# Output product of a recurrent step: the attention output held stationary and the weights moving in two 64-column tiles, instead of the weights held stationary

## The chip, the cores and the metric

The kernel runs on one core of one Trainium2 chip. The metric is device time in microseconds (us) of the whole program. Before the change three runs give a median of 2348.43 us (2343.58 to 2348.47).

## The reference, cut to what matters

Two branches are mixed by a gate. Branch A is sliding-window attention over 2048 tokens of width 640. Branch B is recurrent: it walks through the 2048 tokens in 64 segments of 32, and each segment sees 8 memory tokens that the segment before it made.

```python
g = sigmoid((x * gate_w).sum(-1, keepdims=True))
a = A_ref(x, A_wqkv, A_wo)            # window of 256, 32 heads of 20
mem = mem0                            # 8 tokens of width 640
for s in range(64):                   # branch B
    h = concat([mem, x[32 * s:32 * s + 32]])           # 40 tokens
    q, k, v = h @ Wq, h @ Wk, h @ Wv                   # 32 heads of 192
    p = softmax(mask(q @ k.T * 192 ** -0.5))
    o = (p @ v).reshape(40, 6144) @ Wo                 # 6144 x 640
    mem, b = o[:8], o[8:]
out = g * a + (1 - g) * b
```

## The kernel before, in words

**Stages.** `branch_A` runs first, and while it runs the program begins to load branch B's weights. `tail_projections` then works out, for all segments at once, the part of q, k and v that belongs to the last 8 tokens of each segment and puts it into DRAM (`xin`). What is left for the recurrent loop, `branch_B`, is 32 tokens a step: 8 of memory and 24 of the segment. A step is a chain: everything in it needs the memory that the step before made at its very end.

**Weights.** The four weight matrices of branch B do not fit into SBUF. They are cut into pieces of 128 x 1536 (384 KB), five to each of the four head groups of q, k, v and o. 58 pieces stay in SBUF for the whole loop; the 22 named in `STREAMED` are loaded anew in each step by the SP queue into a ring of six buffers, tag `w`. A buffer is free again when TensorE has used it up.

**A step's work for one head group g (0 to 3).** `chunk` makes q, k and v: the 32 tokens `hT` are stationary in four 32-column tiles, and 384 columns of weights move (line 747). ScalarE copies the result out. `turn` transposes q and k (line 771). GpSimd copies the tail tokens in (`b_K`, `b_Kz`, `b_QT`). `scores` multiplies them (lines 818 and 825), VectorE and ScalarE make the softmax, `turn_p` transposes it (877, 879), `values` multiplies with v (907, 914), and ScalarE copies the result to `OT` (918), which has the head dimension on the partitions and 40 tokens for each of 12 blocks.

**The output product.** `oproj` (line 934) holds a 128 x 128 block of Wo stationary and moves the 40 tokens of `OT` past it: 60 weight loads and 60 products a head group, 240 a step, with the output width on the partitions (`ps_o`, five blocks of 40 tokens). After the last one VectorE copies the 8 memory tokens straight into the next step's `hT` (line 945), since they stand there transposed already. ScalarE copies the other 32 tokens to `oT` (950).

**The rows out.** In the next step, `store` (name `x` in the order) turns `oT` back by five transposes (962), VectorE adds the gated branch A (971), and GpSimd's queue stores the sum (975, 976), loads the rows of branch A for the following segment into the only buffer `ga` (966, 967) and keeps a copy in `b_dram` (964). That load has to wait until the stores before it have landed, and what stands behind it in GpSimd's queue waits with it.

**The order.** TensorE's order within a step is the string `STEP`, written out by hand; q, k, v and o of a group are a word each, `tq`, `tk` the transposes, `s` scores, `p` the transpose of the softmax, `pv` the values. `Sched.run` puts the instructions of all other engines in place by estimated times. The products have a tile mode each: 32 columns (q, k, v, `x`), 64 columns (`tq`, `tk`, `s`, `p`, `pv`), 128 columns (o). The string before changes between modes 19 times a step.

Of the kernel before, what the change touches and what calls it, by code (L numbers as in the profile page):

```python
# [14 lines left out]
SEG = 32  # L15
# [5 lines left out]
def branch_A(tc, x, wqkv, wo, gate_w, ga_dram, spread_x=None, omg_dram=None, omg_sb=None, rl_all=None, exact=False, extra_units=None, W=256, HA=32):  # L21
# [17 lines left out]
    with ExitStack() as ctx:  # L39
# [8 lines left out]
        wq3 = wqkv.rearrange("(kt p) n -> p kt n", p=P)  # L48
# [12 lines left out]
        with tc.tile_pool(name=f"{n_}_wstage", bufs=KT) as wsp:  # L61
# [7 lines left out]
            with nc.allow_non_contiguous_dma(reason="tiny gate vector"):  # L69
                nc.sync.dma_start(gw[:], gate_w.rearrange("(kt p) -> p kt", p=P))  # L70
# [36 lines left out]
        def prep_units(qb):  # L107
            stt = {}

            def u_x():  # L110
                xt = xts.pop(qb)
                tp = ps_p.tile([P, KT, P], BF, name="xT_ps", tag="p")
                for kt in range(KT):
                    nc.tensor.transpose(tp[:, kt, :], xt[:, kt * P:(kt + 1) * P], ident[:])
# [57 lines left out]
        def finish_units(qb):  # L172
# [10 lines left out]
            def u_o(c0, c1):  # L183
# [8 lines left out]
                if c1 == D:  # L192
                    if exact:
                        nc.sync.dma_start(ga_dram[qb * P:(qb + 1) * P, :], ga[:])
                    else:
                        nc.sync.dma_start(ga_dram[:, qb * P:(qb + 1) * P, :].rearrange("k t d -> t k d"), ga[:].rearrange("p (k d) -> p k d", d=P))
# [124 lines left out]
        if omg_dram is not None:  # L321
            with nc.allow_non_contiguous_dma(reason="tiny omg vector"):
                nc.sync.dma_start(omg_dram.rearrange("(b p) -> p b", p=P), omg_all[:])
            for k in range(4):
                for i in range(4):
                    dst = omg_sb[SEG * k:SEG * k + SEG, :].rearrange("p (b i) -> p b i", i=4)[:, :, i]
                    nc.gpsimd.tensor_copy(dst, omg_all[SEG * i:SEG * i + SEG, :])


def mix(tc, b_dram, ga_dram, omg_dram, outf):  # L330
    nc = tc.nc
    nseg = b_dram.shape[0]
    with ExitStack() as ctx:
        one = ctx.enter_context(tc.tile_pool(name="m_c", bufs=1))
        sb = ctx.enter_context(tc.tile_pool(name="m_sb", bufs=2))
        ps = ctx.enter_context(tc.tile_pool(name="m_ps", bufs=2, space=bass.MemoryType.PSUM))
        ident = one.tile([P, P], BF, name="m_ident")
        make_identity(nc, ident[:])
        omg = one.tile([SEG, nseg], FP32, name="m_omg")
        with nc.allow_non_contiguous_dma(reason="tiny omg vector"):  # L340
            nc.sync.dma_start(omg[:], omg_dram[:].rearrange("(s t) -> t s", t=SEG))
        for s in range(nseg):
            bT = sb.tile([P, KT * SEG], BF, name="m_bT")
            nc.sync.dma_start(bT[:], b_dram[s])
            ga = sb.tile([SEG, D], BF, name="m_ga")
            nc.sync.dma_start(ga[:], ga_dram[s * SEG:(s + 1) * SEG, :])
            t = ps.tile([SEG, KT, P], BF, name="m_t")
            for kt in range(KT):
                nc.tensor.transpose(t[:, kt, :], bT[:, kt * SEG:(kt + 1) * SEG], ident[:])
            nc.vector.scalar_tensor_tensor(out=ga[:], in0=t[:].rearrange("p k c -> p (k c)"), scalar=omg[:, s:s + 1], in1=ga[:],  # L350
                                           op0=ALU.mult, op1=ALU.add)
            nc.sync.dma_start(outf[s * SEG:(s + 1) * SEG, :], ga[:])
# [130 lines left out]
class Weights:  # L483


    def __init__(self, tc, Wq, Wk, Wv, Wo, streamed):
        self.tc, self.nc = tc, tc.nc
        self.W = {k: W.rearrange("(kt p) h e -> p kt (h e)", p=P) for k, W in (("q", Wq), ("k", Wk), ("v", Wv))}
# [4 lines left out]
    def load(self, u, dst, engine):  # L493
# [3 lines left out]
        elif m < 4:  # L497
            engine.dma_start(dst, self.Wo[:, 4 * g + m, 0:PIECE])
        else:
            engine.dma_start(dst.rearrange("p (r c) -> p r c", r=4), self.Wo[:, 4 * g:4 * g + 4, PIECE:1920])  # L500

    def load_resident(self, pool, u, engine):
        t = pool.tile([P, PIECE], BF, name=f"w_{u[0]}{u[1]}{u[2]}")
# [9 lines left out]


def o_blocks(m):

    if m < 4:
        return [(m, n // 5, n % 5, n * P) for n in range(12)]
# [612 lines left out]
```

## Time and profile before

| | |
|---|---|
| runs | 2343.58, 2348.43, 2348.47 us |
| the profiled execution | 2344.06 us, span 2342.3 us |
| busy share of the span | PE 86%, PE weight loads 65%, DVE 43%, ACT 39%, POOL 31% |
| mean granted TensorE clock | 0.925 of full speed |
| DMA traffic | 649.24 MB, mean 277 GB/s |
| chain that ended last | PE 67%, DMA 17%, issue 9%, ACT 3%, DVE 3% |
| q, k, v (line 747) on the chain | 23% of the span |
| output product (line 934) on the chain | 17% |

The loop takes the span from about 541 us to its end. A row of a view of groups reads: line, engine, operation, tile written and tiles read, shape, count, then the busy time in us and the mean duration of one in ns, then the idle time of the engine just before them and what ended it. "issue" is time in which the engine waited for nothing that the profile shows. PEclk is the granted TensorE clock as a share of full speed; the DMA share is the mean busy share of the core's 16 DMA engines.

### The profile page before, as it was taken

Reading aid. Unit: us, or ns where it says so; the run is one execution under the profiler, and the core shown is the slowest. Engines: PE = TensorE matmul, PEld = TensorE weight load, DVE = VectorE, ACT = ScalarE, POOL = GpSimd, SP = SyncE. Lnnn points to the kernel's source line nnn. Section 1 sums busy time; section 2 is a strip of 40 time slices with the busy share of each in tenths; the row PEclk is TensorE's granted clock in tenths of the full one; section 3 lists DMA queues with packets and bytes.
Section 4 is the critical chain, followed back from the end, with each engine's and each line's share of the span. In section 5 each row is a group of like instructions: output and inputs, shape, how many; then the busy total and the mean of one; then the engine's idle time right before and its main releaser. Section 6 shows DMA issues by size and latency. Waiting matters only on the chain.

```text
span 2342.3 us, 110323 instructions
## 1 busy us (share of the span) xinstructions
PE 2013.0 (86%) x48566; PEld 1513.0 (65%) x48566; DVE 1014.9 (43%) x3330; ACT 923.1 (39%) x1957; POOL 717.1 (31%) x1957
## 2 busy tenths in 40 slices
PE   6888888997888888888888888888888888888888
PEld 5777777854666666666666666666656666666666
DVE  4666663323444433344444443333334444434334
ACT  3556562223333333333333333333333333333333
POOL 3111121123333333333333333333333333333332
PEclk8778778998999999999999999999999999999999
DMA  3121226558999999999999999999999999999998
GB/s 113 61 67 54 60 63 214 159 170 301 324 329 345 321 336 334 331 329 333 335 333 342 315 335 329 325 326 315 336 313 320 327 328 338 347 316 314 332 332 286
DMA packets 293050, 649.24 MB, mean 277 GB/s; under 512 B 53064, under 2 KB 98768, under 8 KB 292560
## 3 DMA queue, kind: packets, MB, share of 16 engines
q1 hardware_dynamic: 254256, 587.84, 72.0%
q0 software_dynamic: 31392, 47.96, 7.4%
q8 instruction: 382, 6.26, 1.1%
q10 hardware_dynamic: 6912, 6.29, 0.9%
q14 instruction: 108, 0.88, 0.1%
HBM read 612.38 MB, written 29.37 MB: 274 GB/s over the span
## 4 chain that ended last, share of the span: by engine, by line
PE 67%; DMA 17%; issue 9%; ACT 3%; DVE 3%; POOL 0%; SPq 0%; ACTq 0%; POOLq 0%; DVEq 0%
PE ps_o L934 17%; PE ps_k L747 9%; DMA b_w<-in_B_Wv_dram 9%; PE ps_q L747 8%; PE ps_v L747 6%; PE qk_ps L132 5%; PE t_psum L550 4%; DMA b_w<-in_B_Wq_dram 4%; PE ps_pv L907 3%; ACT pt L223 2%; DMA b_w<-in_B_Wo_dram 2%; PE S_ps L825 2%; PE s_ps L220 2%; PE t_psv L573 2%; PE tr_q L771 1%
## 5 line engine op out<-in xcount | busy, mean ns | idle before, releaser
L747 PEld LDWEIGHTS <-b_hT 128*32 128x32 bf16 x15360 | 404.4, 99 | 344.5 <-issue 156.0
L934 PE MATMUL ps_o<-b_OT,w_o 128*128 128x40 bf16 x9984 | 340.0, 182 | 66.3 <-issue 65.9
L934 PEld LDWEIGHTS <-w_o 128*128 128x128 bf16 x9984 | 292.6, 97 | 79.1 <-issue 71.6
L747 PE MATMUL ps_k<-w_k,b_hT 128*32 128x384 bf16 x4352 | 256.8, 346 | 14.8 <-issue 14.5
L803 POOL COPY b_K<-b_xg 128x64 bf16<-128x64 bf16 x256 | 60.1, 235 | 640.8 <-PE S_ps L825 474.4
L747 PE MATMUL ps_v<-w_v,b_hT 128*32 128x384 bf16 x3840 | 240.1, 334 | 13.0 <-issue 12.4
L747 PE MATMUL ps_q<-w_q,b_hT 128*32 128x384 bf16 x3328 | 227.6, 341 | 13.7 <-issue 13.5
L918 ACT CAST b_OT<-ps_pv 128x480 bf16<-128x480 f32 x256 | 143.3, 560 | 232.0 <-PE ps_pv L914 150.2
L934 PE MATMUL ps_o<-b_OT,b_w 128*128 128x40 bf16 x5376 | 196.4, 181 | 44.3 <-issue 40.6
L223 ACT ACTIVATE pt<-s_ps 128x1024 bf16<-128x1024 f32 x180 | 180.8, 1023 | 129.9 <-PE s_ps L220 129.7
L758 ACT CAST b_tok<-ps_q 128x384 bf16<-128x384 f32 x256 | 122.7, 479 | 213.1 <-PE ps_q L747 203.9
L934 PEld LDWEIGHTS <-b_w 128*128 128x128 bf16 x5376 | 164.5, 97 | 49.7 <-issue 44.6
L747 PE MATMUL ps_q<-b_w,b_hT 128*32 128x384 bf16 x1792 | 161.2, 344 | 35.8 <-DVE b_hT L945 18.7
L794 DVE COPY b_K<-tr_k 128x256 bf16<-128x256 bf16 x256 | 72.4, 283 | 272.7 <-PE tr_k L771 268.1
L891 DVE TENSOR_TENSOR b_PTm<-PT_ps,mk_m 128x320 bf16<-128x320 f32 x256 | 125.2, 489 | 140.5 <-PE PT_ps L879 138.8
L758 ACT CAST b_vtok<-ps_v 128x384 bf16<-128x384 f32 x256 | 122.4, 478 | 145.5 <-PE ps_v L747 143.6
L945 DVE CAST b_hT<-ps_o 128x40 bf16<-128x40 f32 x63 | 12.5, 199 | 378.2 <-PE ps_o L934 378.2
L758 ACT CAST b_tok<-ps_k 128x384 bf16<-128x384 f32 x256 | 122.3, 478 | 128.6 <-PE ps_k L747 120.8
L225 DVE TENSOR_TENSOR pt<-pt,pat 128x1024 bf16<-128x1024 bf16 x180 | 124.3, 691 | 75.2 <-ACT pt L223 72.4
L708 POOL DMA_DIRECT2D b_xg<-xin x256 | 137.2, 536 | 62.3 <-POOL b_QT L784 37.9
L836 DVE TENSOR_REDUCE sm<-S_ps 128x4 f32<-128x160 f32 x256 | 80.4, 314 | 140.4 <-PE S_ps L825 139.2
L780 ACT COPY b_QT<-tr_q 128x384 bf16<-128x384 bf16 x256 | 123.7, 483 | 29.6 <-PE tr_q L771 28.9
(137 smaller groups left out, 3738.5 us busy)
## 6 DMA issues: line engine op xcount, KB each, us to landing
b_w<-in_B_Wq_dram SPq DMA_DIRECT2D x448, 384.0 KB, 5.3
b_w<-in_B_Wo_dram SPq DMA_DIRECT2D x448, 384.0 KB, 5.7
b_w<-in_B_Wv_dram SPq DMA_DIRECT2D x320, 384.0 KB, 5.9
b_w<-in_B_Wk_dram SPq DMA_DIRECT2D x192, 384.0 KB, 5.5
xin<-t_qk POOLq DMA_DIRECT2D x8, 1536.0 KB, 9.1
b_xg<-xin POOLq DMA_DIRECT2D x256, 48.0 KB, 5.1
w_k<-in_B_Wk_dram SPq DMA_DIRECT2D x17, 384.0 KB, 4.1
b_xv<-xin POOLq DMA_DIRECT2D x64, 96.0 KB, 5.0
```

The costliest lines, as they stand in the source:

```text
L132: nc.tensor.matmul(pst[:, gg, :], lhsT=Wp[:, kt, 4 * g:4 * g + 4, :].rearrange("p h d -> p (h d)"), rhs=stt['xT'][:, kt, :], start=(kt == ...
L223: nc.scalar.activation(out=pt, in_=sp[:], func=ACT.Exp, scale=scale)
L225: nc.vector.tensor_tensor(out=pt, in0=pt, in1=pat.unsqueeze(1).to_broadcast([P, 2, 512]), op=ALU.min)
L550: nc.tensor.matmul(pt[:, bb, :], lhsT=w[kt][:, c:c + P], rhs=xTb[:, kt, t0:t0 + HS * MEM], start=(x == 0), stop=(x == KT - 1))
L708: sc.op("DMA", 500, lambda: nc.gpsimd.dma_start(tile_of(b)[:].rearrange("p i b t -> p (i b t)"), xin[s, :, c:c + 192]), writes=[b])
L747: nc.tensor.matmul(t[32 * j:32 * j + 32, 0:384], lhsT=tile_of(hT)[:, kt, :], rhs=w[:, j * 384:(j + 1) * 384], start=(kt == 0), stop=(kt == ...
L758: nc.scalar.copy(dst, src)
L780: nc.scalar.copy(dst, tq["tile"][:].rearrange("p b (j t) -> p b j t", t=SEG))
L836: nc.vector.tensor_reduce(out=x["mx"][:], in_=view(), axis=AX.X, op=ALU.max)
L891: nc.vector.tensor_tensor(out=tile_of(PTm)[:], in0=src.to_broadcast([P, 2, 4, L]), in1=mk_m[:].unsqueeze(1).unsqueeze(3).to_broadcast([P, ...
L918: sc.op("ACT", act(480), lambda: nc.scalar.copy(tile_of(OT)[:].rearrange("p b j l -> p (b j l)"), o["tile"][:, 0:480]), reads=[o], writes= ...
L934: nc.tensor.matmul(t[:, dt * L:(dt + 1) * L], lhsT=w_of("o", g, m, wb)[:, c:c + P], rhs=OT["tile"][:, b, i, :], start=(g == 0 and m == 0 a ...
```

## The change

**The output product** is turned over. `OT` is stationary now, 64 columns of it (40 tokens and 24 columns that nobody reads), and 320 columns of Wo move. The two halves of the output width go to the two 64-column tiles of TensorE, so that `ps_o` holds tokens on partitions 0 to 39 and 64 to 103 and 320 columns each. That is 24 products of 320 columns a head group in place of 60 of 40 columns, in the 64-column mode. Wo's pieces are 128 x 1280 now (320 KB), six to a group.

**The memory** no longer stands transposed. VectorE copies all of `ps_o` to `osum` (128 x 320), then TensorE turns the 8 memory tokens by ten products with 8 columns of the identity (`finish`, name `m`, at the end of the step), and VectorE copies the result into `hT`. So that the strided columns `kt::KT` come out right, the rows of Wq, Wk, Wv, of branch A's weights and of x are taken in the order `(p kt)` and not `(kt p)`.

**The rows out** need no transposes: the step `x` with its five transposes, ScalarE's copy to `oT` and one of the two VectorE instructions are gone. One VectorE instruction of 128 x 320 mixes `osum` with `ga`. `osum`, `ga` and the copies are moved by two DMAs of 32 partitions each; the gate `omg_sb` is loaded from DRAM once, by two small DMAs after branch A.

**The order** is a new string with 14 changes of mode a step, and the streamed pieces are others: 14 of 384 KB (q 5, k 4, v 5) and 10 of 320 KB (o), against 22 of 384 KB (q 7, k 3, v 5, o 7).

```diff
-STEP = "q0 k0 k1 tq0 tk0 k2 q1 s0 tk1 tk2 q2 k3 tq1 v0 p0 tq2 s1 q3 v1 s2 tk3 tq3 pv0 v2 p1 s3 o0 pv1 p2 x v3 pv2 p3 o1 pv3 o2 o3"
+STEP = "k0 q0 k1 tk0 tq0 q1 k2 tq1 s0 tk1 k3 q2 s1 tk2 v0 q3 tq2 p0 v1 tk3 pv0 tq3 s2 v2 p1 s3 o0 pv1 p2 v3 pv2 p3 o1 pv3 o2 o3 m"
...
-            for i, b, dt, c in o_blocks(m):
-                nc.tensor.matmul(t[:, dt * L:(dt + 1) * L], lhsT=w_of("o", g, m, wb)[:, c:c + P], rhs=OT["tile"][:, b, i, :],
...
+            for n in range(2):
+                i, b = divmod(2 * m + n, 3)
+                c = (4 * b + i) * L
+                for h in range(2):
+                    w = w_of("o", g, m, wb)[:, n * D + h * (D // 2):n * D + (h + 1) * (D // 2)]
+                    nc.tensor.matmul(t[64 * h:64 * h + 64, 0:D // 2], lhsT=OT["tile"][:, c:c + 64], rhs=w,
...
+                                     tile_position=(0, 64 * h), skip_group_check=True)
...
+        osum = sc.buf("osum")
+        sc.op("DVE", dve(320), lambda: nc.vector.tensor_copy(tile_of(osum)[:], o_b["tile"][:, 0:D // 2]), reads=[o_b], writes=[osum])
...
+            for kt in range(KT):
+                for h in range(2):
+                    nc.tensor.matmul(t[64 * h:64 * h + 64, kt, :], lhsT=osum["tile"][:, kt::KT], rhs=ident[:, 64 * h:64 * h + MEM],
...
+            sc.op("DVE", dve(40), lambda: nc.vector.tensor_copy(tile_of(hT)[:, :, 0:MEM], b["tile"][:]), reads=[b], writes=[hT], after=[xl])
...
+        for h in range(2):
+            sc.op("DMA", 500, lambda h=h: nc.gpsimd.dma_start(half(b_dram, h), mine(osum["tile"], h)), reads=[osum])
+            sc.op("DMA", 500, lambda h=h: nc.gpsimd.dma_start(mine(tile_of(ga), h), half(ga_dram, h)), writes=[ga])
...
+            nc.vector.scalar_tensor_tensor(out=ga["tile"][:], in0=osum["tile"][:], scalar=omg_sb[:, s:s + 1], in1=ga["tile"][:],
...
+        for h in range(2):
+            sc.op("DMA", 500, lambda h=h: nc.gpsimd.dma_start(half(outf, h), mine(ga["tile"], h)), reads=[ga])
...
-            "o": ((3, 4), (1, 3), (1,), (0, 1))}
+            "o": ((0, 3, 5), (0, 3, 5), (0, 5), (3, 5))}
```

On TensorE, where a step ends and the next begins, this stands before (`ps_o` is the output product, `b_hT` the next step's tokens):

```order
L934 LDWEIGHTS w_o_8443
L934 MATMUL ps_o<-b_OT,w_o_8443 128x40
L747 LDWEIGHTS b_hT
L747 MATMUL ps_q<-b_w,b_hT 32x384
L747 LDWEIGHTS b_hT
```

and this at the same place now (`b_osum` is the copied output, `mem_ps` the turned memory; the ten pairs of line 940 are cut to the first):

```order
L920 LDWEIGHTS b_OT_6445
L920 MATMUL ps_o<-b_w,b_OT_6445 64x320
L940 LDWEIGHTS b_osum_6448
L940 MATMUL mem_ps<-ident,b_osum_6448 64x8
...
L729 LDWEIGHTS b_hT
L729 MATMUL ps_k<-w_k_737,b_hT 32x384
```

Ten weight loads and ten products have come between the last output product and the next step's first projection; what is stationary and what moves has changed places. From one step to the next TensorE has 1330 instructions before and 1052 now.

On VectorE the same place reads like this before:

```order
L891 TENSOR_TENSOR b_PTm<-PT_ps,mk_m 128x320
L886 TENSOR_TENSOR b_PTx_6453<-PT_ps,mk_x 64x128
L945 CAST b_hT<-ps_o 128x5x8
L794 COPY b_K_20360<-tr_k 128x8x32
L798 TENSOR_TENSOR b_Kz_6443<-tr_k,mk_z 128x8x32
```

and now:

```order
L873 TENSOR_TENSOR b_PTm<-PT_ps,mk_m 128x320
L868 TENSOR_TENSOR b_PTx_6442<-PT_ps,mk_x 64x128
L928 CAST b_osum_6448<-ps_o 128x320
L954 SCALAR_TENSOR_TENSOR b_ga_6450<-b_osum_6448,omg_sb,b_ga_6450 128x320
L945 CAST b_hT<-mem_ps 128x5x8
L776 COPY b_K_25924<-tr_k 128x8x32
```

The copy into `b_hT` has two instructions of 320 columns ahead of it: the copy to `osum`, and the mix, which needs `ga` from DRAM.

In GpSimd's queue the stores and loads of a step stand together now, at the step's end:

```order
L950 DMA b_dram<-b_osum_6448 32x320
L950 DMA b_dram<-b_osum_6448 32x320
L958 DMA out_dram<-b_ga_6450 32x320
L958 DMA out_dram<-b_ga_6450 32x320
L951 DMA b_ga_6450<-ga_dram 32x320
L951 DMA b_ga_6450<-ga_dram 32x320
L785 COPY b_K_16819<-b_xg 128x8x8
L787 COPY b_Kz_6432<-b_xg 64x4x8
```

The copies behind them are those of head group 2 of the step that has begun, whose buffers come free with that step's `s0`.

165 lines of the change are left out of this document (68 added, 97 removed).

## Prediction

> **What bounds the kernel now.** I begin with the length of a step. VectorE's copy of the memory into `b_hT` ends each step; the view of that line gives its first and last start, and a table by windows gives the busy times between them.
>
> ```profile
> L945 DVE CAST b_hT<-ps_o x63: 198/199/200, 575.9 to 2311.4; 128x40 bf16<-128x40 f32 x63
> ```
> ```profile
> 575.90:2311.40 1735.50, 1493.90 (x41230) 1094.26 (x41230) 710.97 (x2667) 661.69 (x1550) 595.32 (x1673) 0.96 0.95 329
> ```
> ```profile
> 660.95:688.24 27.29, 23.15 (x665) 17.26 (x665) 11.25 (x44) 10.68 (x25) 9.93 (x28) 1.00 0.99 353
> 1981.00:2071.00 90.00, 79.94 (x2212) 58.43 (x2215) 39.87 (x151) 36.60 (x87) 32.45 (x95) 0.96 0.98 343
> ```
>
> The columns are the window, its length, the busy time of PE, PEld, DVE, ACT and POOL, the clock, the DMA share and GB/s. 62 steps take 1735.5 us, 27.99 each, of which PE is busy 24.1. DVE, ACT and POOL are under half busy. The DMA engines are busy 0.95 of it and move 329 GB/s, 9.21 MB a step. So two resources are close together: TensorE with 3.9 us of idle time a step, and the DMA engines with 5%. The second fence is a single step and a 90-us stretch in which the DMA engines did better: 353 and 343 GB/s.
>
> What TensorE's idle time is, the groups of line 934 and the timeline of one output product say.
>
> ```profile
> L934 PE MATMUL ps_o<-b_OT,w_o 128*128 128x40 bf16 x9984 | 340.0, 182 | 66.3 <-issue 65.9
> L934 PE MATMUL ps_o<-b_OT,b_w 128*128 128x40 bf16 x5376 | 196.4, 181 | 44.3 <-issue 40.6 <-DMA b_w<-in_B_Wo_dram 3.2
> ```
> ```profile
> 1455.40 0.42 PE L934 MATMUL ps_o<-b_OT,w_o 128*128 128x40 bf16 x10 [0.55 <-issue]
> ...
> 1459.97 0.39 PE L934 MATMUL ps_o<-b_OT,b_w 128*128 128x40 bf16 x9 [0.49 <-issue]
> 1460.21 0.45 PE L934 MATMUL ps_o<-b_OT,w_o 128*128 128x40 bf16 x12
> 1460.59 0.40 PE L907 MATMUL ps_pv<-b_PTm,b_vtok 128*64 128x160 bf16 x6
> 1460.82 0.26 PE L914 MATMUL ps_pv<-b_PTx,b_xv 128*64 128x64 bf16 x6
> 1461.01 0.47 PE L934 MATMUL ps_o<-b_OT,w_o 128*128 128x40 bf16 x12
> 1461.33 0.45 PE L934 MATMUL ps_o<-b_OT,b_w 128*128 128x40 bf16 x12
> 1461.63 1.06 PE L934 MATMUL ps_o<-b_OT,w_o 128*128 128x40 bf16 x36
> 1462.53 0.76 PE L934 MATMUL ps_o<-b_OT,b_w 128*128 128x40 bf16 x24
> 1463.13 0.43 PE L934 MATMUL ps_o<-b_OT,w_o 128*128 128x40 bf16 x11
> 1465.63 0.79 PE L934 MATMUL ps_o<-b_OT,w_o 128*128 128x40 bf16 x25 [2.07 <-issue]
> ```
> ```profile
> q1 hardware_dynamic: 254256, 587.84, 72.0%
> ...
> q8 instruction: 382, 6.26, 1.1%
> ```
>
> Line 934 loses 65.9 + 40.6 = 106.5 us to "issue", 1.66 a step, and waits only 3.2 us for its weights. From the stall that ended at 1459.97 to the one that ended at 1465.63 TensorE ran 9+12+6+6+12+12+36+24+11 = 128 products, in the middle of a weight piece and of a block. Queue q8 carries 382 packets; TensorE has 48,566 products and as many loads, so a packet is 254 instructions: the 128 products with their loads. I read the stalls as TensorE having run through its block of instructions before the next had come through the crowded DMA engines. From stall to stall 5.66 us passed, 3.59 of them work: the fetch takes longer than 128 products of 40 columns do. The stall ahead of these ended at 1455.40, so the block in between took 4.57 us with a stall of 0.49: the fetch takes some 4.5 to 5.7 us.
>
> The stalls cost a second time.
>
> ```profile
> 1463.00:1466.40 3.40, 1.33 (x48) 1.15 (x44) 0.00 (x0) 0.00 (x0) 0.52 (x1) 0.99 1.02 366
> 1466.40:1469.80 3.40, 3.11 (x41) 1.61 (x44) 0.20 (x1) 0.77 (x2) 1.26 (x3) 0.50 0.74 221
> ```
>
> After 2.07 idle us in 3.4, the next 3.4 us have half the clock, and DMA falls to 0.74 as well, since buffers are not freed. A mean clock of 0.96 over the loop means 8% of it at half clock: up to 0.04 x 27.99 = 1.1 us of TensorE's time a step.
>
> **The change part by part**, us a step, TensorE's side first. The chain of waits gives the pieces:
>
> ```profile
> 1423.01 0.21 PE ps_pv L907 x6
> ...
> 1432.38 1.60 PE ps_o L934 x60
> ...
> 1437.53 0.02 issue
> 1437.55 0.21 DVE b_hT L945
> 1437.76 0.04 issue
> ...
> 1441.61 0.29 PE tr_q L771 x6
> 1441.90 0.17 PE tr_k L771 x6
> 1442.07 0.93 PE ps_k L747 x20
> 1443.00 0.81 PE ps_q L747 x20
> ...
> 1456.89 0.21 PE ox_ps L962 x5
> ```
>
> (a) *The output product itself.* Before, 60 products take 1.60, so 240 take 6.4. Now 48 pairs of 320 columns. Line 747 moves 384 columns in four tiles at once at 0.81/5 = 0.162 a group of four, which scales to 0.135 for 320; line 907 moves a pair of 160 in 0.07, which scales to 0.14. So 6.5 to 6.7: **+0.15** (0 to +0.3).
>
> (b) *Instruction stalls in it.* TensorE goes from 1330 to 1052 instructions a step, but what counts is the place: 128 products of the new shape last 64 x 0.135 = 8.6 us, longer than the fetch of 4.5 to 5.7. The 1.66 should go almost wholly: **-1.6** (0 to -1.66). The stalls elsewhere stay, since q, k, v and the scores run as before. [...]
>
> (c) *The half clock.* Part of the 1.1 goes with the stalls that bring it. The new pause at the step's end, (f), is shorter than the 2.07 above, but may sometimes do the same: **-0.6** (0 to -1.1).
>
> (d) *Mode changes.* `tr_q` behind `ps_k` takes 0.29, `tr_k` behind `tr_q` 0.17, `ps_k` behind a transpose 0.93, `ps_q` behind it 0.81: 0.12 a change. 19 become 14: **-0.6**.
>
> (e) *The five transposes* of line 962 go: **-0.2**.
>
> (f) *The end of the step*, where nothing else can run, because every product of the next step needs `hT`. Now 0.02 + 0.21 + 0.04 = 0.27 pass. The new chain is the copy of 128 x 320, the ten products, and then the same 0.27. The nearest rows:
>
> ```profile
> L891 DVE TENSOR_TENSOR b_PTm<-PT_ps,mk_m 128x320 bf16<-128x320 f32 x256 | 125.2, 489 | 140.5 <-PE PT_ps L879 138.8
> ...
> L805 POOL COPY b_Kz<-b_xg 64x32 bf16<-64x32 bf16 x512 | 106.2, 207 | 15.1
> ...
> L784 POOL COPY b_QT<-b_xg 128x96 bf16<-128x96 bf16 x256 | 67.3, 263 | 15.8
> ...
> L803 POOL COPY b_K<-b_xg 128x64 bf16<-128x64 bf16 x256 | 60.1, 235 | 640.8 <-PE S_ps L825 474.4 <-DMA b_xg<-xin 77.8 <-PE ps_o L934 20.5
> ...
> L976 POOL DMA_DIRECT2D out_dram<-b_ga x64 | 32.4, 506 | 1.7 <-issue 1.7
> ...
> L971 DVE SCALAR_TENSOR_TENSOR b_ga<-ox_ps,omg_sb,b_ga 128x128 bf16<-128x128 bf16 x64 | 21.9, 342 | 5.9 <-DMA b_ga<-ga_dram 5.3 <-PE ox_ps L962 0.5
> ...
> L191 DVE TENSOR_SCALAR ga<-out_ps,gcol 128x320 bf16<-128x320 f32 x32 | 17.4, 545 | 2.5 <-PE out_ps L189 2.4
> ```
>
> The copy costs about 0.5 (line 891: 489 ns; line 191: 545). The ten small products cost, from line 962 doubled, 0.4, with the way through the array and the semaphores about 0.6. The mix of 128 x 320 stands on VectorE between the two copies; at about 0.5 (342 ns for 128 columns, 489 to 545 for other instructions of 320) it runs beside the ten products and is covered; without that cover it would add 0.5. Together **+1.1** (+0.7 to +1.6). The mix also needs `ga`, whose load was issued a step earlier.
>
> GpSimd's queue: two copies to `b_dram`, two stores, then two loads that wait until the stores have landed, and behind them the tail copies for head group 2, for which `s2` waits.
>
> ```profile
> DMA to landing us min/median/max: 3.3/5.0/6.7
> ```
>
> That is the row of line 976's stores. Six issues of 0.5 (line 976, also 32 partitions), a landing of 5.0 and copies of 0.235 + 2 x 0.207 + 0.263 = 0.9 are 8.9 us, and with the 0.5 of the copy to `osum` they end 9.4 us into the step, 11.1 with a landing of 6.7. Ahead of `s2` stand 1.4 us of (f), ten projections of 0.81, six transposes of 0.17 and nine changes of 0.12, 11.6 us without the scores and values between them: covered, so nought (up to +0.3).
>
> Sum: 0.15 - 1.6 - 0.6 - 0.6 - 0.2 + 1.1 = -1.75: TensorE alone would allow 26.2.
>
> *The DMA's side.* Streamed weights go from 22 x 384 = 8448 KB to 14 x 384 + 10 x 320 = 8576 KB, +0.13 MB; instructions fall by 278 x 64 bytes (6.26 MB over 97,132), -0.02. Demand 9.32 MB a step. At 329 GB/s that is 28.3 us, at 343 27.2, at 353 26.4. Each is above TensorE's 26.2, so the DMA is late next: the gain of 1.75 is cut. I take 343, the rate of a stretch of three steps, since TensorE will hold the ring up less: **27.2**, 0.79 less than now, 64 x 0.79 = 51 us.
>
> Outside the loop I count nought: branch A's strided transposes are as many as before, and the small gate loads stand in GpSimd's queue where it was idle. Allow 5 us either way.
>
> The profiled execution took 2344.06 us, 2342.3 of them the span. 2344 - 51 = 2293; the median of the runs is 4.4 above that execution, so I forecast 2296.
>
> **The rivals.**
>
> *The DMA stays at its share (slower).* Place: the end of each step, where the ring of six fills while nothing is freed for 1.4 us. If the mean rate stays at 329 GB/s, a step is 28.3: +0.3 x 64 = +20, 2368. It decides where the rate stays under 9.32 MB / 27.99 us = 333. For it: the share is 0.95 already, and more bytes are asked for. Against: the windows show the share falling after TensorE's stalls, to 0.74, and 0.98 to 0.99 in good stretches. Chance 0.11.
>
> *The stalls are not the fetch (slower).* [...] Against it stand the 128 products. Chance 0.03.
>
> *The two column tiles don't run together (slower).* Then 96 x 0.135 = 13.0: 26.2 + 6.5 = 32.7, +300 us. Line 907's pairs, also in two tiles, speak against it. Chance 0.01.
>
> *Half the gain.* The rate rises to 337 GB/s only: 27.65, 2326. Chance 0.17; within 0.2% of now, 0.05.
>
> *The DMA gives way further.* At 353 GB/s as in the one step: 26.4, 2246. Chance 0.10. My forecast's own case (2275 to 2315) has 0.53.
>
> **How the numbers follow.** About 0.2% (4.7 us) is what a measurement of this kernel tells from no change. Faster: 0.53 + 0.17 + 0.10 = 0.80; same 0.05; slower 0.15. The range leaves out the slower cases (0.15) and the lower half of the last: 2262 to 2345.
>
> **What would show it.** Right: "issue" at the output product under 0.3 us a step, the loop's clock at 0.98, the DMA share at 0.97 or more with waits for weights in place of the stalls, and 1.3 to 1.5 us between the last output product and `ps_k`. Wrong: "issue" as large as now there; a rate at 329 GB/s; PE waiting for GpSimd's copies at `s2`; half-clock windows after each step's end.

## The result, and the profile after

| | before | changed |
|---|---|---|
| median (lowest to highest) | 2346.01 us (2337.42 to 2348.47, 4 runs) | 2273.48 us (2252.83 to 2276.28, 4 runs) |
| profiled execution, span | 2344.06 us, 2342.3 us | 2252.83 us, 2251.1 us |
| mean granted clock over the span | 0.925 | 0.952 |

The ratio is 0.9675, 95% interval 0.9621 to 0.9729, so 3.2% faster by the ratio; the medians lie 73 us apart. The forecast was 2296, the range 2262 to 2345. The profiled execution is the fastest of the four; the other three took 2271 to 2276, and a fifth execution on record, which is not in the median, took 2265.15.

The length of a step comes from the same two views as before, the line that ends a step and the table by windows over the loop (window, length, busy time of PE, PEld, DVE, ACT and POOL, clock, DMA share, GB/s):

```profile
L945 DVE CAST b_hT<-mem_ps x63: 198/199/201, 583.4 to 2219.2; 128x40 bf16<-128x40 f32 x63
```
```profile
583.40:2219.20 1635.80, 1479.65 (x32612) 1074.06 (x32612) 732.23 (x2666) 652.86 (x1488) 597.98 (x1736) 1.00 0.99 353
```

62 steps take 1635.8 us, 26.38 each, where they took 27.99. The clock rose from 0.96 to 1.00, the DMA share from 0.95 to 0.99, the rate from 329 to 353 GB/s; 353 x 26.38 is 9.3 MB a step, as forecast. So the DMA engines are full now. The loop gave back 1735.5 - 1635.8 = 99.7 us; the part ahead of the first `b_hT` became longer by 583.4 - 575.9 = 7.5, the part behind the last by 1.0, which leaves the 91.2 between the two profiled executions.

On the profile's page of the changed kernel, the instruction queue, the chain and the groups of the output product say what changed places:

```profile
q8 instruction: 313, 5.13, 0.9%
...
PE 54%; DMA 36%; DVE 4%; ACT 3%; issue 3%; POOL 0%; SPq 0%; ACTq 0%; DVEq 0%; POOLq 0%
...
L920 PE MATMUL ps_o<-b_w,b_OT 128*64 128x320 bf16 x2560 | 298.5, 301 | 49.8 <-DMA b_w<-in_B_Wo_dram 44.1
L920 PE MATMUL ps_o<-w_o,b_OT 128*64 128x320 bf16 x3584 | 330.0, 299 | 0.4 <-issue 0.3
```

"issue" ahead of the output product was 106.5 us; here it is 0.3 in one group, and the list of waits below has 3.0 for both. In its place stand 44.1 us of waiting for streamed pieces of Wo, where 3.2 stood. On the chain, issue went from 9% to 3% and DMA from 17% to 36%. The same in the list of TensorE's waits between 600 and 2150 us (total us, times, longest). First the kernel before, the larger of its waits for "issue", at the output product and elsewhere:

```profile
PE ps_o L934 <- issue: 95.4, 74, 2.6
...
PE ps_q L747 <- issue: 14.8, 14, 2.5
PE ps_k L747 <- issue: 14.3, 17, 1.5
...
PE ps_v L747 <- issue: 12.8, 14, 2.1
...
PE ps_pv L914 <- issue: 9.6, 6, 2.1
```

And the changed kernel, from the top of its list:

```profile
PE ps_o L920 <- DMA b_w<-in_B_Wo_dram: 41.2, 67, 1.9
PE mem_ps L940 <- DVE b_osum L928: 34.4, 59, 0.6
PE ps_v L729 <- DMA b_w<-in_B_Wv_dram: 19.1, 40, 1.3
PE ps_k L729 <- DVE b_hT L945: 17.5, 59, 0.3
PE ps_q L729 <- DMA b_w<-in_B_Wq_dram: 10.2, 18, 1.3
PE S_ps L807 <- issue: 4.6, 9, 1.1
...
PE ps_v L729 <- issue: 3.4, 6, 1.0
PE ps_o L920 <- issue: 3.0, 5, 1.3
PE ps_q L729 <- issue: 1.3, 2, 0.8
```

Waits for weights and the two waits of the step's end lead the list; waits for "issue" are single rows of a few us. What the reader should also see is in the lower rows of the first of these two fences: before, the projections and values lost 14.8 + 14.3 + 12.8 + 9.6 = 51.5 us to "issue" too (68.8 with the smaller rows elsewhere that are not shown), and most of that has gone as well, though those products themselves were not changed.

The end of a step, on the chain of waits (start, length, what):

```profile
1427.48 3.46 PE ps_o L920 x48
1430.94 0.02 issue
1430.97 0.50 DVE b_osum L928
1431.47 0.04 issue
1431.51 0.57 PE mem_ps L940 x7
1432.08 0.02 issue
1432.11 0.21 DVE b_hT L945
1432.32 0.04 issue
1432.36 1.00 PE ps_k L729 x20
```

From the last output product to the next projection 1.42 us pass, and the projections behind it run at full clock (20 products in 1.00; the granted clock is 1.00 from 1432.49 to 1435.90).

### The profile page after: what moved, and what is told of

It reads as the page before. It is cut to its first block, busy times and chain, and to the rows that moved or that the text cites. A ratio compares the mean times of both kernels' runs of the same rounds, so it can differ in the third digit from the quotient of the medians.

```text
span 2251.1 us, 92658 instructions
## 1 busy us (share of the span) xinstructions
PE 1995.3 (89%) x39670; PEld 1488.7 (66%) x39670; DVE 1036.5 (46%) x3330; ACT 914.3 (41%) x1893; POOL 717.5 (32%) x2011
## 4 chain that ended last, share of the span: by engine, by line
PE 54%; DMA 36%; DVE 4%; ACT 3%; issue 3%; POOL 0%; SPq 0%; ACTq 0%; DVEq 0%; POOLq 0%
DMA b_w<-in_B_Wo_dram 14%; DMA b_w<-in_B_Wv_dram 12%; PE ps_o L920 10%; PE ps_k L729 8%; DMA b_w<-in_B_Wk_dram 8%; PE ps_v L729 6%; PE ps_q L729 5%; PE qk_ps L132 5%; PE t_psum L538 4%; ACT pt L220 3%; PE S_ps L807 2%; PE tr_k L753 2%; PE tr_q L753 2%; PE s_ps L217 2%; PE ps_pv L889 1%
## 5 line engine op out<-in xcount | busy, mean ns | idle before, releaser
L729 PEld LDWEIGHTS <-b_hT 128*32 128x32 bf16 x15360 | 378.9, 97 | 291.4 <-issue 91.0
L920 PEld LDWEIGHTS <-b_OT 128*64 128x64 bf16 x6144 | 398.4, 110 | 78.6 <-issue 73.1
L920 PE MATMUL ps_o<-b_w,b_OT 128*64 128x320 bf16 x2560 | 298.5, 301 | 49.8 <-DMA b_w<-in_B_Wo_dram 44.1
L920 PE MATMUL ps_o<-w_o,b_OT 128*64 128x320 bf16 x3584 | 330.0, 299 | 0.4 <-issue 0.3
L729 PE MATMUL ps_q<-w_q,b_hT 128*32 128x384 bf16 x3840 | 237.0, 330 | 1.3 <-issue 1.3
L729 PE MATMUL ps_v<-w_v,b_hT 128*32 128x384 bf16 x3840 | 228.1, 328 | 2.3 <-issue 2.1
L776 DVE COPY b_K<-tr_k 128x256 bf16<-128x256 bf16 x256 | 73.3, 286 | 289.3 <-PE tr_k L753 288.4
L928 DVE CAST b_osum<-ps_o 128x320 bf16<-128x320 f32 x64 | 31.5, 492 | 351.5 <-PE ps_o L920 351.5
L753 PEld LDWEIGHTS <-b_tok 128*64 128x64 bf16 x3072 | 101.1, 110 | 94.1 <-ACT b_tok L740 40.9
L950 POOL DMA_DIRECT2D b_dram<-b_osum x128 | 64.4, 507 | 273.4 <-DVE b_osum L928 266.2
L951 POOL DMA_DIRECT2D b_ga<-ga_dram x128 | 63.8, 498 | 263.8 <-DMA out_dram<-b_ga 255.8
```

Source lines behind the costliest of these rows:

```text
L729: nc.tensor.matmul(t[32 * j:32 * j + 32, 0:384], lhsT=tile_of(hT)[:, kt, :], rhs=w[:, j * 384:(j + 1) * 384], start=(kt == 0), stop=(kt == ...
L753: nc.tensor.transpose(t[64 * a:64 * a + 64, k, :], tok["tile"][:, c:c + 64], ident[:], tile_position=(0, 64 * a))
L920: nc.tensor.matmul(t[64 * h:64 * h + 64, 0:D // 2], lhsT=OT["tile"][:, c:c + 64], rhs=w, start=(g == 0 and m == 0 and n == 0), stop=(g == ...
```

## The experiments

The theory: TensorE ran out of instructions, because 128 products of 40 columns, a block with their loads, last less than the fetch of the next block (3.59 us against an estimate of 4.5 to 5.7); longer products cure that, and then the bytes that the DMA engines must move set the step. The rivals: the gain comes from the smaller number of mode changes, the new order or the shorter end of the step; or the DMA engines were the bound all along and gave way for another reason. The diffs below are cut to the lines that carry each edit; lines that only follow from them are left out.

### The stalls alone: the old kernel with wide products

`b_wide` is the kernel before, with 24 output products of 160 columns a head group in place of 60 of 40. Each of the first four or five blocks of a piece is held, and 160 columns of `OT` move past it: most of Wo is loaded but left out of the sum, and the bytes, the order, the mode and the end of the step stay as they were.

```diff
-            for i, b, dt, c in o_blocks(m):
-                nc.tensor.matmul(t[:, dt * L:(dt + 1) * L], lhsT=w_of("o", g, m, wb)[:, c:c + P], rhs=OT["tile"][:, b, i, :],
+            for n in range(4 if m == 4 else 5):
+                d = L * (n % 2)
+                nc.tensor.matmul(t[:, d:d + 4 * L].rearrange("p (j l) -> p j l", l=L), lhsT=w_of("o", g, m, wb)[:, n * P:(n + 1) * P], rhs=OT["tile"][:, n % 3, :, :],
```

> The kernel before, with its weights still stationary, but 24 products of 160 columns a head group in place of 60 of 40: the same 128 x 128 loads in kind, 2400 moving columns in place of 2400 (60 x 40 = 2400; 24 x 160 = 3840, at 67 ns each 1.6 us, as long as the 60 take), 1042 instructions a step in place of 1330. It leaves out most blocks of Wo, so its output is not the reference's. Nothing else of the change is in it: old order, old pieces, old end of the step, 19 changes of mode. Theory (TensorE runs out of fetched instructions in the output product): the stalls there go and the half clock with them, the step is bounded by its DMA, 9.2 MB at 345 to 355 GB/s, 26.0 to 26.7 us, 2240 to 2280 in all. Rival (the gain came from the new order and the fewer changes of mode): 2330 to 2350, with the issue time at the output product as before.

Measured: 2184.52 us (2179.72 to 2185.85), ratio 0.9324 (0.9301 to 0.9347). Its loop by windows, the two longest waits at the output product, and 48 of its products on the chain:

```profile
574.80:2150.70 1575.90, 1473.99 (x32302) 1089.80 (x32302) 710.54 (x2666) 662.69 (x1550) 594.46 (x1671) 1.00 1.00 362
```
```profile
PE ps_o L935 <- DMA b_w<-in_B_Wo_dram: 10.8, 15, 1.9
PE ps_o L935 <- issue: 4.0, 8, 0.7
```
```profile
1438.11 3.44 PE ps_o L935 x48
```

The expectation's first count of the columns is a slip: 24 products of 160 columns move 3840 columns a head group, not 2400. With the old bytes, mode, order and end of step, nearly all of the stalls and of the half clock are gone, and the DMA engines are at 1.00. A step takes 1575.9/62 = 25.42 us. TensorE's products take about as long as they did (48 in 3.44 us, so 96 in 6.9, where 240 took 6.4); only their number fell. The stalls, with the half clock that they bring, are enough to explain the whole gain of the change, and more. The time lies below the 2240 to 2280 of the theory, which had taken 345 to 355 GB/s where 362 came.

### The products cut again

`e_split4` and `e_split2` are the changed kernel with each product of 320 columns cut into four of 80 or two of 160; the sums are the same.

```diff
-                for h in range(2):
-                    w = w_of("o", g, m, wb)[:, n * D + h * (D // 2):n * D + (h + 1) * (D // 2)]
-                    nc.tensor.matmul(t[64 * h:64 * h + 64, 0:D // 2], lhsT=OT["tile"][:, c:c + 64], rhs=w,
+                for d in range(0, D // 2, 80):
+                    for h in range(2):
+                        w = w_of("o", g, m, wb)[:, n * D + h * (D // 2) + d:n * D + h * (D // 2) + d + 80]
+                        nc.tensor.matmul(t[64 * h:64 * h + 64, d:d + 80], lhsT=OT["tile"][:, c:c + 64], rhs=w,
```

> The changed kernel with each product of 320 columns cut into four of 80: the same columns, the same weights and result, 768 instructions of output product a step in place of 192 (1628 a step in all). Theory (fetch): 128 products now last 64 x 0.035 = 2.2 us against a fetch of 4.5 to 5.7, three blocks a step stall 2 to 3 us each, of which the weights' waits hide about 1.4, and the half clock comes back: 30 to 35 us a step, 2500 to 2850. Rival (what counts is the columns, the mode and the order): the pairs of 80 columns stream as fast as those of 320 and the time stays at 2270, at most 2300.

Measured: 2632.81 us (2618.62 to 2636.05), ratio 1.1223 (1.1182 to 1.1263). Its wait at the output product, its loop, and a piece of the chain:

```profile
PE ps_o L921 <- issue: 202.9, 127, 4.6
```
```profile
596.40:2594.30 1997.90, 1597.31 (x50468) 1178.27 (x50468) 736.21 (x2667) 651.50 (x1488) 596.16 (x1736) 0.93 0.88 290
```
```profile
1441.24 1.73 PE ps_o L921 x96
...
1443.60 2.63 issue
```

The timeline shows where that stall falls (start, length, products, idle time ahead of them):

```profile
1442.52 0.46 PE L921 MATMUL ps_o<-b_w,b_OT 128*64 128x80 bf16 x16
...
1443.26 0.34 PE L729 MATMUL ps_v<-w_v,b_hT 128*32 128x384 bf16 x3
1446.23 1.46 PE L729 MATMUL ps_v<-w_v,b_hT 128*32 128x384 bf16 x13 [2.63 <-issue]
```

Behind 96 short products it is the projection of v that stands still for 2.63 us: the run of short products had used up its block, as I read it, and the instruction that came first in the next one waited. That is how stalls at lines that the change doesn't touch can belong to the output product. The products between the stalls are no slower than before they were cut: 1.73 us for 96 is 6.9 for a step's 384, and 96 of 320 columns take 6.9 too. So the weight loads, four times as many, cost nothing here but the stalls.

> The changed kernel with each product of 320 columns cut into two of 160: 384 instructions of output product a step in place of 192 (1244 a step in all). Theory (fetch): 128 products last 64 x 0.07 = 4.5 us, about as long as the fetch at its quickest, so stalls of 0 to 1 us at 1.5 blocks a step, which the waits for weights mostly hide: 2270 to 2320. Rival (stalls go by the number of instructions alone): 1244 lies 69% of the way back from 1052 to 1330, so 69% of the gain is lost, 2320 to 2330.

Measured: 2306.74 us (2299.74 to 2310.99), ratio 0.9856 (0.9833 to 0.9879). Wait, loop and 48 products:

```profile
PE ps_o L921 <- issue: 27.1, 33, 1.9
```
```profile
583.90:2264.20 1680.30, 1493.17 (x38564) 1098.80 (x38564) 735.17 (x2666) 650.63 (x1488) 595.90 (x1736) 0.99 0.97 344
```
```profile
1443.26 1.80 PE ps_o L921 x48
```

The four lengths together. The time of 128 products is scaled from the chain (1.73 x 128/96, 1.80 x 128/48, 3.46 x 128/48); for the kernel before it is the 3.59 of the prediction. "issue" a step is the row of waits over the number of steps in 1550 us:

| kernel | columns, products a step | 128 products last | "issue" at the output product, a step | us a step |
|---|---|---|---|---|
| e_split4 | 80 in pairs, 384 | 2.3 us | 202.9 / 48.1 = 4.2 us | 32.2 |
| before | 40, 240 | 3.6 us | 95.4 / 55.4 = 1.7 us | 28.0 |
| e_split2 | 160 in pairs, 192 | 4.8 us | 27.1 / 57.2 = 0.5 us | 27.1 |
| changed | 320 in pairs, 96 | 9.2 us | 3.0 / 58.7 = 0.05 us | 26.4 |

In these four kernels the stalls are the larger the less 128 products last: 4.2 us a step at 2.3 us, 0.05 at 9.2. The forecast's fetch of 4.5 to 5.7 us, an estimate, fits: at 4.8 us the stalls are few, at 9.2 all but gone. The columns alone don't say it: `e_split4` moves 80 to an instruction where the kernel before moves 40, but two of them run at once (a pair of 160 takes 1.80/24 = 0.075 us in `e_split2`, a single product of 160 3.44/48 = 0.072 in `b_wide`), so that 128 last less, and it is the slower of the two.

The instruction queue itself shows whose wait it is. In the kernel before, 149 stalls of over 0.3 us between 600 and 2300 us are put down to "issue", 176.7 us in all; 72 of them, 73.3 us, stand at other lines than the output product. Each of the 149 ended between 1.2 and 1.6 us after a packet of q8 had come in (0.9 to 1.7 us for the 167 of `e_split4`). And q8's packets keep step with TensorE's products: the stalls lie on one line of 127.6 products to a packet, none more than one product off it. Where two stalls stand one block apart, 63 times, their ends lie 4.0 to 6.6 us apart, 5.5 on the median, which I take as an estimate of the time of a fetch. So the stalls at the projections and values are the same wait.

### The end of the step

`e_nochain` leaves the recurrence out: no `m` in the order, no ten products, no copy into `hT`, so that the memory tokens of a step don't depend on the step before.

```diff
-... pv2 p3 o1 pv3 o2 o3 m"
+... pv2 p3 o1 pv3 o2 o3"
...
-                    nc.tensor.matmul(t[64 * h:64 * h + 64, kt, :], lhsT=osum["tile"][:, kt::KT], rhs=ident[:, 64 * h:64 * h + MEM],
...
-            sc.op("DVE", dve(40), lambda: nc.vector.tensor_copy(tile_of(hT)[:, :, 0:MEM], b["tile"][:]), reads=[b], writes=[hT], after=[xl])
```

> The changed kernel without the end of the step: no products that turn the memory and no copy into the next step's tokens, so that a step does not wait for the one before. It leaves out the recurrence, so the output is not the reference's. Theory (the DMA is the bound now): the weights come no faster, 9.32 MB at 355 GB/s are 26.2 us against 26.4, so 2255 to 2275, and TensorE waits for weights where it waited for the memory. Rival (the 1.4 us at the step's end are on the path): 64 x 1.4 = 90 us less, 2180 to 2200.

Measured: 2264.81 us (2260.35 to 2273.04), ratio 0.9676 (0.9645 to 0.9708), the same ratio as the change's. Its longest wait, in the window of before:

```profile
PE ps_q L729 <- DMA b_w<-in_B_Wq_dram: 53.1, 98, 2.1
```

The pause of 1.4 us went, and the waits for Wq rose from 10.2 to 53.1 us, which is most of what the two rows of the step's end (34.4 + 17.5) had been. So the longer end of the step costs at most the 9 us between the two medians, and not the 90 of the rival: TensorE has to wait for the weights, at one place or another.

`e_gap2` and `e_gap` make that end longer, by making the copy to `osum` twice or three times; the diff is that of `e_gap`.

```diff
-        sc.op("DVE", dve(320), lambda: nc.vector.tensor_copy(tile_of(osum)[:], o_b["tile"][:, 0:D // 2]), reads=[o_b], writes=[osum])
+        for _ in range(3):
+            sc.op("DVE", dve(320), lambda: nc.vector.tensor_copy(tile_of(osum)[:], o_b["tile"][:, 0:D // 2]), reads=[o_b], writes=[osum])
```

> The changed kernel with the copy of the output to SBUF made three times in a row, so that the end of each step lasts 1.0 us longer. Theory (the DMA is the bound, and the end of the step is paid from TensorE's 1.4 us of waits for weights): at most 0.4 us a step, 2270 to 2300. Rival (the end of the step is on the path): 64 us more, 2335.

> The changed kernel with the copy of the output to SBUF made twice, so that the end of each step lasts 0.5 us longer (half of what the run with three copies added, which cost 71 us, with 41 of its windows of 3.4 us at half clock). Theory (the pause itself is paid from the waits for weights, and the cost is the half clock, which comes where about 1.8 us of a window of 3.4 are idle): the idle time per step stays under that in most steps, 5 to 25 us more than the changed kernel, 2278 to 2300. Rival (the pause is on the path by its length): half of 71, 2305 to 2312.

Measured: `e_gap` 2344.27 us (2327.13 to 2354.0, 10 runs), ratio 1.0005 (0.997 to 1.0041); `e_gap2` 2296.28 us (2290.66 to 2303.65), ratio 0.9834 (0.9767 to 0.9902). The theory's number for `e_gap` was missed by far, and the rival's 2335 is the nearer: a microsecond more at the end of the step takes the whole gain away. Two windows of it, 3.41 us each, and the chain there:

```profile
1249.24:1252.65 3.41, 1.59 (x24) 0.95 (x18) 2.10 (x5) 0.00 (x0) 0.42 (x1) 1.00 1.03 401
1252.65:1256.06 3.41, 3.23 (x44) 1.61 (x48) 0.12 (x1) 0.48 (x1) 1.55 (x4) 0.50 0.87 294
```
```profile
1251.99 0.56 PE mem_ps L941 x10
...
1252.83 1.79 PE ps_k L729 x15
1254.62 1.59 PE ps_q L729 x15
1256.21 0.81 PE ps_k L729 x18
```

In the first window TensorE is idle for 3.41 - 1.59 = 1.82 us; in the next its clock is 0.50, 15 products take 1.79 where 18 take 0.81 afterwards, and the DMA share falls to 0.87. The clock over `e_gap`'s loop is 0.96 as it was in the kernel before, and its rate 336 GB/s. The steps one by one part the pause from the half clock. In `e_gap2`, 44 of the 62 steps have no half clock in them and take 26.41 us on the mean, as long as the 59 such steps of the changed kernel (26.36); the other 18 take 28.39. In `e_gap`, 22 steps without it take 26.86 and 40 with it 28.25. So half a microsecond of pause is covered by the DMA's lateness, a whole one only in part, and the larger cost is the half clock. The change's own 1.4 us are just short of that: +0.5 us costs 2296.28 - 2273.48 = 23 us, or 23/63 = 0.36 a step, +1.0 us costs 71, or 1.12 a step.

### The bytes

`e_fewer` and `b_fewer` take two streamed pieces of Wo from resident ones instead (other values in the sum): 2 x 320 KB a step less for the changed kernel, 2 x 384 KB less for the kernel before.

```diff
+SAME = {("o", 0, 3): ("o", 0, 1), ("o", 1, 3): ("o", 1, 1)}
...
-            "o": ((0, 3, 5), (0, 3, 5), (0, 5), (3, 5))}
+            "o": ((0, 5), (0, 5), (0, 5), (3, 5))}
```

> The changed kernel with two of its ten streamed pieces of Wo left out (each time a piece that lies in SBUF is used in their place, so part of the output product is not the reference's): 0.66 MB a step less, the same instructions. Theory (the DMA is the bound now): 8.67 MB at 353 GB/s are 24.5 us, less than the 25.0 that TensorE needs without its 1.4 us of waits for weights, so 25.0 to 25.5 us a step against 26.4 and 2185 to 2220 in all. Rival (TensorE is the bound): not under 2255.

> The kernel before with two of its seven streamed pieces of Wo left out (a piece in SBUF is used in their place, so part of the output product is not the reference's): 0.79 MB a step less, the same instructions. Theory (the stalls for instructions bind there, and the DMA is only close): the 0.5 us of waits for weights go, the fetch gets a little quicker on DMA engines that are less crowded, 26.7 to 27.5 us a step against 28.0, 2260 to 2315 in all. Rival (the DMA was the bound already): 8.42 MB at 329 GB/s are 25.6 us, 2190.

Measured: `e_fewer` 2193.91 us (2190.41 to 2208.1), ratio 0.9399 (0.9328 to 0.9471); `b_fewer` 2307.23 us (2297.56 to 2317.52), ratio 0.9861 (0.9783 to 0.9938). The loop of each by windows, first `e_fewer`, then `b_fewer`:

```profile
584.60:2156.80 1572.20, 1438.40 (x32612) 1079.68 (x32612) 729.30 (x2667) 650.64 (x1488) 596.24 (x1736) 1.00 0.97 342
```
```profile
578.40:2276.30 1697.90, 1477.70 (x41230) 1090.50 (x41230) 715.43 (x2667) 662.72 (x1550) 598.41 (x1672) 0.97 0.91 308
```

And the longest of `b_fewer`'s waits:

```profile
PE ps_o L934 <- issue: 73.4, 61, 3.2
```

In the changed kernel 7% fewer bytes bring the step from 26.38 to 1572.2/62 = 25.36 us: bytes bound it. In the kernel before 9% fewer bring it from 27.99 to 27.39, and the DMA share falls to 0.91: there they were not the bound by themselves. The stalls are what is left of the wait, 73.4 us in place of 95.4. That the fetch got quicker, as was expected, does not show: the ends of stalls one block apart lie 5.4 us apart on the median, where it was 5.5. `e_fewer` also shows that TensorE alone would allow 25.4 us or less.

`e_ring5` has five buffers in the ring of streamed pieces instead of six, and keeps one piece of Wq more in SBUF.

```diff
-RING = 6
+RING = 5
...
-STREAMED = {"q": ((2, 4), (), (1, 4), (1,)),
+STREAMED = {"q": ((2, 4), (), (4,), (1,)),
```

> The changed kernel with five ring buffers in place of six, and the room used for one more piece of Wq that stays in SBUF: 23 pieces and 8.93 MB a step in place of 24 and 9.32. Theory (bytes bound it, and five buffers keep the DMA engines busy): 8.93 MB at 353 GB/s are 25.3 us, 1.1 less a step, 2200 to 2225 in all. Rival (the number of pieces in flight sets the rate): it falls by up to a sixth, 300 to 340 GB/s, 26.3 to 29.8 us, 2270 to 2490.

Measured: 2313.62 us (2307.28 to 2326.33), ratio 0.9899 (0.9822 to 0.9976). Its loop, and its longest wait:

```profile
585.70:2277.80 1692.10, 1494.40 (x32612) 1072.46 (x32612) 731.96 (x2666) 649.91 (x1488) 595.76 (x1736) 1.00 0.96 327
```

```profile
PE ps_o L920 <- DMA b_w<-in_B_Wo_dram: 68.7, 121, 1.8
```

The theory fell and the rival was right: 8.9 MB a step (327 x 27.29) take longer than 9.3 did. The clock is 1.00 and TensorE waits for weights (68.7 us for Wo's in the window where it was 41.2); the rate itself fell from 353 to 327 GB/s with one buffer less in the ring.

`e_full` loads the streamed pieces of Wo 1536 columns wide, the extra ones unused.

```diff
-            engine.dma_start(dst, self.Wo[:, r, c // 2:c // 2 + 2 * D])
+            n = dst.shape[-1]
+            engine.dma_start(dst, self.Wo[:, r, c // 2 + (2 * D - n if c else 0):c // 2 + (2 * D if c else n)])
...
-                sc.op("SP", 0.65 * weights.width(kind), lambda b=b, u=u: weights.load(u, tile_of(b)[:, 0:weights.width(u[0])], nc.sync), writes=[b])
+                sc.op("SP", 0.65 * weights.width(kind), lambda b=b, u=u: weights.load(u, tile_of(b)[:], nc.sync), writes=[b])
```

> The streamed pieces of Wo are loaded whole, 1536 columns wide where the changed kernel leaves out the columns that it keeps for good; the extra columns are never used and the output is the reference's. The demand grows by about 0.66 MB to 9.98 MB a step, every piece on its way is now 384 KB, and nothing changes for TensorE. What is asked is the rate. Theory (the rate is set by the bytes on their way in the six buffers, which were 6 of 366 KB on the mean before and are 6 of 384 KB now; five buffers gave 327 in place of 353 GB/s): 361 to 363 GB/s, as in the old kernel with the wide products, 27.6 us a step and 2335 to 2355 us in all. Rival (353 GB/s is what the queue gives this kernel, whatever is on its way): 28.3 us a step and 2375 to 2395 us in all. Either way the time grows by the bytes, since the DMA engines are the bound; a time under 2300 us would say that they are not.

Measured: 2326.09 us (2317.35 to 2332.29), ratio 0.9925 (0.9896 to 0.9954). Its loop, and the row of the weights' queue over the loop; behind it the same row of the changed kernel:

```profile
582.70:2290.50 1707.80, 1507.80 (x32614) 1076.12 (x32612) 734.99 (x2667) 650.27 (x1488) 596.03 (x1736) 0.99 0.99 362
```
```profile
q1 hardware_dynamic: 214448, 585.67, 92.7%
```
```profile
q1 hardware_dynamic: 214318, 544.70, 91.6%
```

A step takes 1707.8/62 = 27.55 us at 362 GB/s, as the theory said (its total was 9 to 29 us too high; it was reckoned from the changed kernel's median, which lies 21 us above its profiled execution). The rate rose to that of `b_wide`. Why is less sure than the number. The queue moved 585.67 MB in 0.927 x 16 x 1707.8 = 25,330 us of engine time, 23.1 KB per us, against 544.70 in 0.916 x 16 x 1635.8 = 23,974, or 22.7. So 1.8% come from engines that move more in the same time, and 1.2% from engines that are busy more of it. More bytes on their way and longer rows (3072 bytes a partition in place of 2560) are both candidates; no run parts them.

### The order, and the rows of the weights

`e_order` has the old order string (without `x`, with `m` at its end) in the changed kernel; `e_kt` loads the rows of Wq, Wk and Wv in the old order `(kt p)`, so that they meet the wrong rows of `hT`.

```diff
-STEP = "k0 q0 k1 tk0 tq0 q1 k2 tq1 s0 tk1 k3 q2 s1 tk2 v0 q3 tq2 p0 v1 tk3 pv0 tq3 s2 v2 p1 s3 o0 pv1 p2 v3 pv2 p3 o1 pv3 o2 o3 m"
+STEP = "q0 k0 k1 tq0 tk0 k2 q1 s0 tk1 tk2 q2 k3 tq1 v0 p0 tq2 s1 q3 v1 s2 tk3 tq3 pv0 v2 p1 s3 o0 pv1 p2 v3 pv2 p3 o1 pv3 o2 o3 m"
```
```diff
-        self.W = {k: W.rearrange("(p kt) h e -> p kt (h e)", p=P) for k, W in (("q", Wq), ("k", Wk), ("v", Wv))}
+        self.W = {k: W.rearrange("(kt p) h e -> p kt (h e)", p=P) for k, W in (("q", Wq), ("k", Wk), ("v", Wv))}
```

> The changed kernel with the words of the order string as they stood before (q0 first, tk2 ahead of q2, and so on; x left out, m at the end). Changes of mode stay 14, the streamed pieces stay. Theory (the gain is the output product's shape and the bytes bound the rest): within 1% of the changed kernel, 2255 to 2300. Rival (the new order carries the gain): back by half of it or more, 2310 to 2345.

> The changed kernel with the rows of Wq, Wk and Wv taken in the order (kt p) as before, so that the 128 rows of a piece lie 12 KB apart in DRAM and not 60 KB. The contraction then pairs wrong rows, so the output is not the reference's; pieces, bytes and instructions are the same. Theory (bytes and stalls set the time, not where the rows lie): no difference, 2260 to 2285. Rival (the wider spread costs the DMA rate, which would be why the changed kernel moves 353 GB/s and the kernel before with wide products 362): 2215 to 2235.

Measured: `e_order` 2288.68 us (2276.97 to 2298.61), ratio 0.9788 (0.9712 to 0.9864); `e_kt` 2270.05 us (2266.06 to 2272.19), ratio 0.9706 (0.9642 to 0.977). The new order is worth some 15 us, with intervals of the ratios that just overlap; against `e_kt`, which was run alongside it, it is 19 us, and there the runs do not overlap. The order of the rows is worth nothing that can be told.

## Why the prediction was right, and where it was not

**What bounds the kernel.** Right. The stalls were the fetch, and the DMA engines came next. The stalls at the output product took 1.7 us a step where 128 of its products last 3.6 us, and 0.05 in the changed kernel, where they last 9.2.

**(a) The product, +0.15.** Mis-sized: 48 products of 320 columns took 3.46 us on the chain, so 96 take 6.9, +0.5 to the 6.4 of before. The scaling from 384 and 160 columns was too kind. It cost nothing, because TensorE is not last. The same holds for the misses on TensorE's side that follow: they were hidden by the DMA's side.

**(b) Stalls, -1.6.** Right at the output product (1.72 a step to 0.05). "The stalls elsewhere stay" was the step that failed: all rows elsewhere lost 68.8/55.4 = 1.24 us a step before, and 11.4/58.7 = 0.19 now. It is not the new order: in `b_wide`, with the old one, the four rows that made 51.5 us make 7.2. `e_split4` shows how: the stall of a run of short products can fall on the projection behind it, 2.63 us on that of v.

**(c) Half clock, -0.6.** The clock of the loop is 1.00, so nearly the whole of the 1.1, itself an upper bound, went.

**(d), (e)** were not measured alone. The new order as a whole is worth about 15 us in `e_order`, with a DMA that hides part of it.

**(f) The end of the step, +1.1.** Right in length: 1.42 in place of 0.27, of it 0.50 for the copy and 0.57 for the products (in the forecast's 0.6, the 0.2 for the way through the array and the semaphores was the author's estimate; no run shows it apart). It was counted as a cost to TensorE's side, and with the weights late it is nearly free (`e_nochain`). The half clock, named as a danger of this pause, came in only three of the loop's windows of 3.41 us; `e_gap2` and `e_gap` show that it was near.

**GpSimd's queue, nought.** Right: TensorE has no wait for its copies in the whole list. (Eight groups of transposes stand ahead of `s2` in the new string, not six, which makes the cover 11.9 us and not 11.6.)

**TensorE alone, 26.2.** Too high: `e_fewer` runs a step in 25.36, and about 1 us of that is still waits for weights. With 1.24 - 0.19 = 1.05 more from (b), 0.5 more from (c) and 0.35 less from (a), the sum of -1.75 becomes -2.95, and 27.99 - 2.95 = 25.0. An estimate from the changed kernel agrees: its waits for weights are 41.2 + 19.1 + 10.2 + 4.1 = 74.6 us, 1.27 a step, and 26.38 - 1.27 = 25.1.

**The DMA's side, 27.2.** The demand was right (9.3 MB). The rate was the term of the sum that was mis-sized: 343 was taken, 353 came, the rate of the one good step, and 26.4 us a step with it. That was the rival of "gives way further", at a chance of 0.10; its total of 2246 is near the profiled execution's 2253. The 343 came from a stretch that still held stalls; it was not a limit of the DMA engines. Against 27.2 a step this made 63 x 0.8 = 50 us. The start of the program, counted at nought, took back 7.5 of them. If the 20 us between the median and the profiled execution lie in the loop, the median's steps are (2273 - 2253)/63 = 0.3 us longer, or 26.7; no trace of those executions shows it, but `e_kt`, 2272.19 us in its profiled execution, has steps of 1650.2/62 = 26.6 at 350 GB/s. So the median lies between the forecast's case and that rival. The last addition is a slip too: 2293 + 4.4 is 2297, not 2296.

**The rivals.** The slower one by the DMA's share did not come, since the share rose to 0.99. That the stalls are not the fetch is ruled out by the table of four lengths and by the packets of q8; that the two tiles don't run together, by 48 products in 3.46 us.

What stays open: why the changed kernel's queue gives 353 and not the 362 GB/s of `b_wide` and `e_full` (of the causes named, only the order of the rows is ruled out); and how much of the gain the mode changes and transposes have.

## What to carry to other kernels

Look at the products' length in time, not at their columns: where a block of TensorE's instructions was used up faster than the next came through busy DMA engines (3.6 us against some 5.5), fewer and longer instructions won here even with 3840 columns a head group in place of 2400 (`b_wide`, ratio 0.9324). When a stall goes, take the rate of the next resource from a stretch without that stall, even a short one (here 353 GB/s, the rate that came), and not from a long stretch that still holds it (343). A pause at a point where nothing else can run may be free by its length, where another resource is late anyway, and still dear if it is long enough to halve the clock: with half a microsecond more, steps of `e_gap2` took 26.41 us without the half clock, against 26.36, and 28.39 with it.

## What the hardware showed that was not expected

**Half the clock came after less than 3.41 us of idle time.** In the loop of the kernel before the clock changed only on a grid of 3.41 us: 35 of its stretches at half clock last 3.41 us and five last 6.83; the three of the changed kernel last 3.41 each. Counted over the loop in windows on that grid: in the kernel before each of 25 windows with at least 1.8 us idle was followed by one at half clock, 10 of 15 with 1.5 to 1.8 and 6 of 27 with 1.2 to 1.5; in `e_gap` 32 of 32, and 7 of 23 with 1.5 to 1.8. So 1.8 us within one window were enough in all 57 windows of those two kernels. It is no sharp limit: the changed kernel has a window with 1.91 us idle, from 2003.06 us, and `e_full` two with 1.95 that no half clock followed.

**The rate fell with the number of buffers in the ring.** Five gave 327 GB/s, six 353, with the clock at 1.00 in both, and TensorE waiting for weights. How many of the buffers were being filled at a time was not measured.
